# Residual and last tokens' phases of four batches turned on TensorE, with a new order of the whole program

## The chip, the cores and the metric

The kernel runs on one core of a Trainium2 chip. The metric is the device time of one execution in microseconds; lower is better. The engines are TensorE (PE in the profile), VectorE (DVE), ScalarE (ACT), GpSimd (POOL) and SyncE (SP), which here issues all transfers. Each works through its own queue in order.

## What is computed

An attention over 8 batches, 8 heads, 576 tokens and 64 channels a head, followed by a token-mixing block of width 512. Cut to what matters:

```python
q_d, k_d, v_d = means of q, k, v over groups of 4 tokens      # 144 tokens
out_d = softmax(q_d @ k_d.T / 8) @ v_d                        # repeated 4 times
out_local = softmax of q @ k.T / 8 where |i - j| < 4, @ v
x = out_up + out_local                                        # [8, 576, 512]

theta = x @ w_theta
zr, zi = x * cos(theta), x * sin(theta)
y = w_tok_r @ zr + w_tok_i @ zi                               # over tokens
u = x + y
out = u + maximum(u @ w_ch, 0)
```

## The kernel before

The program is written as small steps, each a function of a batch and a part, and the text `ORDER` names them one after the other: two letters for the step, then a place (a PSUM bank or a pair of banks, a staging buffer, or the engine: `v` VectorE, `a` ScalarE, `g` GpSimd). The loop at the end of the kernel walks over the words; each word takes the next instance of its step, so that the order within a step is fixed and the interleaving of steps is the text's. `pin` ties every instruction to the one before it on the same engine: the text is the order of every engine's queue. Eight batches go through it as a pipeline, with two buffers for most tiles. A word `wm` issues so many idle matmuls on a tile of zeros into a bank; they compute nothing.

The steps, in the order in which a batch meets them:

- `lk`, `lq`, `lv`/`lw` (L278, L330): loads of k, q and the two halves of v into one of 14 staging buffers. `ck`, `cq`, `cv` (L287, L341): their casts to bf16. `la`/`ca`, `lb`/`cb`, `lc`/`cc`, `wp`/`wc`: the weights.
- `tp` (L294): transposes of k and q on TensorE into a pair of banks; `ev` (L298): the copy out, into `kT`, `qT`.
- `kd`, `qd` (L304 to L318): the sums over 4 tokens. `sd`, `ed`, `nd`, `xn`, `xd`, `xc`: the coarse attention.
- `ps`, `ex`, `mk`, `po`, `nm` (L427 to L465): scores, exponential, mask, product with v and division of the local attention, in units of 116 tokens.
- `xt`, `xa` (L475, L481): x with channels on the partitions, `xT`.
- `th` (L492): theta of 128 tokens; `cs` (L497): cosine and sine. `tt`, `ct`: the same for the last 64 tokens, with channels on the partitions. `zt` (L513): their product with x, in `zT`.
- `dz` (L517): a transposing transfer turns `zT` into `z[:, 8, :]`, where tokens are on the partitions.
- `xm` (L523): x of 128 tokens turned on TensorE into a bank. For the batches in `XDMA`, here 6 and 7, `dx` (L526) does it by a transposing transfer into `xx`. `zz` (L530): x times cosine and sine, into `z`.
- `mx` (L546): the mixing over tokens, nine matmuls of 288 columns into a bank; `ua` (L551): plus x, into `uT`.
- `du` (L555): four transposing transfers a batch turn `uT` into `ur`, the residual with tokens on the partitions. `ut`, `dt`: the same for the last tokens of two batches.
- `ch` (L563): `u @ w_ch` of 128 tokens; `rl` (L568): the maximum with 0, plus `ur`, into one of five output buffers; `st` (L572): the store. `ht`, `rt`, `ss`, `sr`: the last tokens of two batches.
- `te`, `ts` (L643): a tiny activation that brings the table of exponential or sine onto ScalarE ahead of its use.

All matmul results lie in eight PSUM banks, which the words name.

Of the kernel before, what the change touches and what calls it, by code (L numbers as in the profile page):

```python
# [14 lines left out]
P = 128  # L15
B = 8
# [3 lines left out]
DM = 512  # L20
# [33 lines left out]
lb5 lb4 cba cbg cbg xn xt0 la6 lb7 cag nd67 la8 xt1 mk xn lb9 wm24 xd6 lba wp7 lbb lqc xca xt2 nm xt3 po45 cqg cbv caa  # L54
lkd xa lk0 caa wp6 ckg xa xa nm xm0 wca wp1 lq2 lk3 th7 ts cs cbg xa wcv xt2 lk5 th4 xa wp5 cbv tt3 xm2 cba ckg xm6 zz
wcv th7 cs wp4 xm0 zz ct wp1 lq4 tp23 wcv lq1 wp5 wcv lk7 cs cqv zt eva lq6 dz ckg th4 cs wp7 wcv wcv wp1 lq8 ckv zz
cqg lvc cqg wcv tp23 wcv tp45 tp67 eva kdg zz ckg mx1 lka eva mx0 cqv cqg ua eva ps23 lw kdv te ex ckg qdv ps45 ua lvb
ex mx1 mk tp67 tp23 lkd eva lk9 lw lv0 eva lw lv3 lv2 mx0 cvv po45 lw ua qdg ps67 mk lw mx1 nm cva ckg lq5 ckg tp23 ex
ua po45 kdv cvg nm sd67 eva ed lq4 mx0 sd23 qdg cva po45 ua cqg cqg ua nm mx6 cva lq1 lk6 ua lv7 mk pv01 kdg po45 wm71
po67 ed tp23 lk8 nm vda lva nm eva cka nd45 nd01 xt6 ps23 xn cqv qdg ckg lw cvg ps45 xn ex lqc mx7 lw lqd mk ua ps23  # L60
lk9 xd0 ex sd45 xt1 ex xcv xa ed cqg lvb tp23 xt0 xa xa ckg xt7 xt6 lk0 xa po45 cqg eva xa lw th1 ts cs xm0 tp23 tt7
th6 lq3 ct lv2 nm xm1 evv th4 xm5 lw th7 cs cs zt zz zz lv5 ckg xm6 dz tp23 cs eva cqv tp01 zz cvg po45 zz utg lk4 mk
mx7 mx6 qdg cvg po23 lw nm eva ua ps01 sd45 mx7 kdg lc6 ua te ed xt6 cvv ex mk nm cvg ua pv45 vda mk ps23 cka po01 lk1
lq8 nm mx7 kdg nd45 nd01 ua ex mx7 xn qdg lv7 lvc sd23 xn ps45 lw ua lc9 mk lw lvd lw lv0 du lva ed lw xt0 lw cvg xd1
xcv mx7 lq3 xa xt1 lcb ckg ex lk5 lc2 du xa xt4 cvg xa cca tp23 mx5 cva ua lv4 xa lq7 sd01 cqg ua eva cvg po67 nm po23
nm mx4 ed xt5 ua po01 th6 xa th7 nm ccv lk1 ts cs du po23 nm po45 du cqg cvg pv01 nm th6 xm2 tt3 ccg vda nd45 zz ckg
ct xn nd01 th2 xn cs tp45 ccv ckg xt3 xt7 zt xd0 lqc ch1 eva xcv cqg cs xa lw xa cqa xm0 xm4 lk8 kdg lk6 lvd lk0 lw
lk3 dz xt5 lka ch3 lvb tp67 cvg lw rl lq5 lq9 eva cs st ch1 xa rl zz ckv th5 ckg xt0 utv du du du du tp67 cs xm3 eva
cka zz th2 xa kdv mk ch0 cs zz th4 tp67 rl mx5 mx1 evv cs ps23 lq1 qdg ua po67 rl ua lv7 lv2 lq4 nm ps45 mx0 cqg xm1
cqv te ex xt6 xm7 mx2 lw mk ex ua ckg st cvg lw zz tp45 eva qdg tp01 xa tt3 mx6 mk zz th7 ua lk6 ts ct evv ua cvv lvc  # L70
lv8 xm2 cs lw lw zt ckg lv5 lw po45 sd01 cqa qdg lq0 ch3 ch6 nm st rl zz rl te ed xm7 mx3 du cvg zz cva ch2 dz ps45
# [21 lines left out]
def kernel(  # L93
# [11 lines left out]
    nc = tc.nc  # L105
# [40 lines left out]
    rl = tiles(2, [P, 2, 4], "rl", FP32)  # L146
# [23 lines left out]
    ident = one([P, P], "ident")  # L170
# [86 lines left out]
    at = {}  # L257
# [258 lines left out]
    def dz(b, w):  # L516
        nc.sync.dma_start_transpose(out=z[b % 2][:, 8, :].rearrange("p (e d) -> p e d", e=4),  # L517
                                    in_=zT.rearrange("p e r t -> p (e r t)"))

    def xm(b, c, w):  # L520
        ps = at["xm", b, c] = bank16(w)[:, 0:DM]
        for dc in range(4):
            nc.tensor.transpose(out=ps[:, P * dc:P * dc + P], in_=xT[b % 2][:, dc, P * c:P * c + P], identity=ident)  # L523
# [4 lines left out]
    def zz(b, c, w):  # L528
        x = xx[:, c, :] if b in XDMA else at.pop(("xm", b, c))
        nc.vector.tensor_tensor(out=z[b % 2][:, 2 * c:2 * c + 2, :],  # L530
# [22 lines left out]

    def du(b, dc, w):
        nc.sync.dma_start_transpose(out=ur[b % 2][:, :, P * dc:P * dc + P], in_=uT[b % 2][:, dc, 0:512])  # L555

    def ut(b, w):
        COPY[w](out=uts[b // 2 % 2][:, :, b % 2, :], in_=uT[b % 2][:, 0:4, 512:576])  # L558
# [35 lines left out]
    def span(*ns):  # L594
        out = [()]
        for n in ns:
            out = [x + (i,) for x in out for i in range(n)]
        return out

    STEPS = dict(  # L600
        k0=(lambda i, w: None, span(1)), kc=(kc, span(4)), la=(la, span(4)), ca=(ca, span(4)), lb=(lb, span(9)), cb=(cb, span(9)), lc=(lc, span(4)), cc=(cc, span(4)),
# [8 lines left out]
        zt=(zt, span(B)), dz=(dz, span(B)), xm=(xm, [(b, c) for b, c in span(B, 4) if b not in XDMA]), dx=(dx, [(b, c) for b, c in span(B, 4) if b in XDMA]), zz=(zz, span(B, 4)), mx=(mx, span(B, 8)),  # L610
        ua=(ua, span(B, 8)), du=(du, span(B, 4)), ut=(ut, span(B)), ch=(ch, span(B, 4)), rl=(rlf, span(B, 4)),
# [69 lines left out]
```

## Time and profile before

| | us |
|---|---|
| runs | 245.91, 248.43, 248.76 |
| median | 248.43 |
| the profiled execution | 247.32 |
| its span, first to last instruction | 245.6 |

| transfers, KB each | number | median us from issue to landing |
|---|---|---|
| halves of v, 128 | 80 | 5.6 |
| k, 288 | 32 | 5.4 |
| q, 288 | 32 | 4.8 |
| `du` | 32 | 3.8 |
| `dz` | 8 | 3.0 |
| `dx` | 8 | 2.5 |
| stores of output, 256 | 32 | 2.8 |

"Busy" sums the time in which an engine had an instruction; matmuls overlap in a pipeline, so that TensorE can be busy without being at its peak. A line names the line of the kernel, the engine, the tile written and the tiles read, with partitions and elements. In square brackets stands the idle time ahead of an instruction and what ended it. "issue" means that the profile shows nothing that the engine waited for. The chain of waits follows the work that ended last back to its releasers.

### The profile page before, as it was taken

To read this page: it belongs to the slowest core of one execution; us is meant where nothing else is said; L and a number is where in the kernel's file an instruction comes from. 1 tells how busy PE (TensorE), PEld (TensorE's weight loads), DVE (VectorE), ACT (ScalarE), POOL (GpSimd) and SP (SyncE) were. 2 spreads that over 40 slices of the span, in tenths; PEclk is the share of its full clock that TensorE was granted. 3 is DMA by queue.
4 is the path that set the end of the run, shared out by engine and by line. 5 is a ranking of instruction groups with operands and counts; after the bars stand their busy time and mean duration, and the time that the engine had idled before them with its cause. 6 is when DMAs were issued, how large, how long until landed. Compare 5 with 4: busy or idle time off the path is not lost.

```text
span 245.6 us, 8335 instructions
## 1 busy us (share of the span) xinstructions
PE 224.6 (91%) x3405; PEld 153.3 (62%) x3405; DVE 196.7 (80%) x410; ACT 155.7 (63%) x237; POOL 97.7 (40%) x143
## 2 busy tenths in 40 slices
PE   7998699797999789999988999999599999999992
PEld 2555467566777557686566687576367775677740
DVE  6479798797999879999878998888498888576472
ACT  3287598896997487988765579885756536800000
POOL 6361366569577353637078142119334000000000
PEclk9999999999999999999999999999999999999999
DMA  6999997899969999998999999899956395655577
GB/s 188 300 180 293 380 342 177 205 262 248 221 109 251 122 256 236 250 291 201 204 184 237 283 262 164 172 234 234 154 117 154 93 161 153 115 129 119 140 202 268
DMA packets 87494, 50.91 MB, mean 207 GB/s; under 512 B 72480, under 2 KB 72480, under 8 KB 87456
## 3 DMA queue, kind: packets, MB, share of 16 engines
q1 hardware_dynamic: 87456, 50.38, 92.9%
q8 instruction: 26, 0.43, 0.9%
q14 instruction: 12, 0.10, 0.1%
HBM read 34.11 MB, written 9.44 MB: 177 GB/s over the span
## 4 chain that ended last, share of the span: by engine, by line
PE 49%; DMA 21%; DVE 7%; ACT 7%; issue 5%; POOL 5%; SPq 4%; DVEq 0%; POOLq 0%; ACTq 0%
PE PS L546 17%; DMA st<-in_v_dram 13%; PE PS L563 8%; PE PS L492 7%; DMA st<-in_q_dram 4%; PE PS L294 3%; PE PS L638 3%; DMA st<-in_moe_w_tok_i_dram 3%; SPq L330 3%; POOL two L312 3%; PE PS L475 2%; PE PS L456 2%; DVE osb L568 1%; ACT cs L498 1%; ACT pm L435 1%
## 5 line engine op out<-in xcount | busy, mean ns | idle before, releaser
L546 PE MATMUL PS<-WT,z 128*128 128x288 bf16 x576 | 77.6, 286 | 1.7 <-DMA z<-zT 1.2
L546 PEld LDWEIGHTS <-z 128*128 128x128 bf16 x576 | 54.3, 98 | 17.0 <-DMA z<-zT 1.8
L551 DVE TENSOR_TENSOR uT<-PS,xT 128x288 bf16<-128x288 f32 x64 | 28.7, 452 | 13.7 <-PE PS L546 12.1
L492 PE MATMUL PS<-wth,xT 128*128 128x512 bf16 x128 | 32.1, 379 | 2.9 <-DVE osb L568 2.8
L563 PE MATMUL PS<-wch,uT 128*128 128x512 bf16 x128 | 31.1, 379 | 0.0
L465 DVE TENSOR_TENSOR tmp<-PS,rl 128x512 bf16<-128x512 f32 x40 | 27.7, 691 | 1.4
L568 DVE SCALAR_TENSOR_TENSOR osb<-PS,ur 128x512 f32<-128x512 f32 x32 | 21.8, 685 | 8.4 <-issue 3.6
L497 ACT ACTIVATE cs<-PS,pihc 128x512 bf16<-128x512 f32 x32 | 22.3, 697 | 9.0 <-PE PS L492 8.5
L341 POOL CAST v_w<-st 128x512 bf16<-128x512 f32 x22 | 14.2, 649 | 34.5 <-DMA st<-in_v_dram 34.3
L481 DVE TENSOR_TENSOR xT<-PS,xdT 128x464 bf16<-128x464 f32 (+1 forms) x40 | 23.8, 628 | 1.8 <-PE PS L475 1.7
L435 ACT ACTIVATE pm<-PS 128x1024 bf16<-128x1024 f32 (+1 forms) x24 | 20.5, 877 | 2.6 <-PE PS L427 2.5
L287 POOL CAST k_tm<-st 128x576 bf16<-128x576 f32 x19 | 13.2, 699 | 19.0 <-DMA st<-in_k_dram 18.9
L298 ACT COPY qT<-PS 128x1152 bf16<-128x1152 bf16 x14 | 15.8, 1131 | 7.5 <-PE PS L294 7.3
L558 POOL COPY ut<-uT 128x256 bf16<-128x256 bf16 x5 | 2.2, 437 | 45.4 <-DVE uT L551 45.4
L492 PEld LDWEIGHTS <-xT 128*128 128x128 bf16 x128 | 11.3, 98 | 13.5 <-issue 3.4
L312 POOL TENSOR_TENSOR two<-kT 128x580 f32<-128x580 bf16 x13 | 15.4, 1184 | 10.1 <-DVE kT L298 9.8
L643 ACT ACT_TABLE_LOAD x15 | 19.2, 1283 | 0.3
L498 ACT ACTIVATE cs<-PS 128x512 bf16<-128x512 f32 x32 | 19.4, 605 | 0.0
L563 PEld LDWEIGHTS <-uT 128*128 128x128 bf16 x128 | 11.8, 98 | 11.2
L382 ACT ACTIVATE pd<-PS 128x864 bf16<-128x864 f32 x16 | 14.0, 891 | 6.5 <-PE PS L371 6.4
L446 DVE TENSOR_TENSOR pm<-pm,band 128x1024 bf16<-128x1024 bf16 (+1 forms) x24 | 16.7, 696 | 1.3 <-ACT pm L435 1.3
L530 DVE TENSOR_TENSOR z<-PS,cs 128x1024 bf16<-128x1024 bf16 x24 | 16.2, 681 | 1.4 <-ACT cs L498 1.3
(95 smaller groups left out, 401.7 us busy)
## 6 DMA issues: line engine op xcount, KB each, us to landing
st<-in_v_dram SPq DMA_DIRECT2D x80, 128.0 KB, 5.6
st<-in_k_dram SPq DMA_DIRECT2D x32, 288.0 KB, 5.4
st<-in_q_dram SPq DMA_DIRECT2D x32, 288.0 KB, 4.8
out_dram<-osb SPq DMA_DIRECT2D x32, 256.0 KB, 2.8
st<-in_moe_w_tok_r_dram SPq DMA_DIRECT2D x4, 288.0 KB, 5.5
st<-in_moe_w_tok_i_dram SPq DMA_DIRECT2D x4, 288.0 KB, 6.6
st<-in_moe_w_theta_dram SPq DMA_DIRECT2D x4, 256.0 KB, 6.6
st<-in_moe_w_ch_dram SPq DMA_DIRECT2D x4, 256.0 KB, 4.5
```

The lines of the kernel that those rows point to most:

```text
L312: nc.gpsimd.tensor_tensor(out=t, in0=src[:, :, 0:2], in1=src[:, :, 2:4], op=ALU.add)
L435: nc.scalar.activation(out=pm[(3 * b + u) % NPM][:, :, 0:n].rearrange("p e c j w -> p e (c j w)"), in_=at.pop(("ps", b, u))[:, :, 0:4 * W ...
L465: nc.vector.tensor_tensor(out=tmp[(NCH * b + c) % NTMP].rearrange("p g (j d) -> p g j d", d=D), in0=ps[:, :, :, 0:D], in1=r.unsqueeze(3).t ...
L481: nc.vector.tensor_tensor(out=xT[b % 2][:, :, CH * c:CH * c + cnt].rearrange("p e (m j) -> p e m j", j=4), in0=at.pop(("xt", b, c))[:, :, ...
L492: nc.tensor.matmul(out=ps, lhsT=xT[b % 2][:, dc, P * c:P * c + P], rhs=wth[:, dc, :], start=(dc == 0), stop=(dc == 3))
L497: nc.scalar.activation(out=t[:, 0, :], in_=ps, func=AF.Sin, bias=pihc, scale=1.0)
L498: nc.scalar.activation(out=t[:, 1, :], in_=ps, func=AF.Sin, bias=0.0, scale=1.0)
L546: nc.tensor.matmul(out=ps, lhsT=z[b % 2][:, j, P * dc:P * dc + P], rhs=WT[:, j, cols], start=(j == 0), stop=(j == 8))
L551: nc.vector.tensor_tensor(out=uT[b % 2][:, dc, cols], in0=at.pop(("mx", b, i)), in1=xT[b % 2][:, dc, cols], op=ALU.add)
L563: nc.tensor.matmul(out=ps, lhsT=uT[b % 2][:, dc, P * c:P * c + P], rhs=wch[:, dc, :], start=(dc == 0), stop=(dc == 3))
L568: nc.vector.scalar_tensor_tensor(out=o, in0=at.pop(("ch", b, c)), scalar=0.0, in1=ur[b % 2][:, c, :], op0=ALU.max, op1=ALU.add)
L643: nc.scalar.activation(out=idle, in_=pihc, func=TABLE[kind])
```

## The change

There are four edits.

- `RPE = (0, 1, 2, 3)`: for these batches the residual `ur` is made by `up`, four TensorE transposes into a bank for each 128 tokens, and `uc`, the copy out of it, instead of the four `du` transfers of the batch.
- `ZPE = (0, 1, 2, 3)`: for these batches the last tokens' phases are turned by `zp`, four TensorE transposes, and `zc`, a copy, instead of `dz`.
- `XDMA = (7,)`: x of batch 6 is turned by `xm` on TensorE; only batch 7 still uses `dx`.
- `ORDER` is another text throughout: 1219 words for 1198. It holds 68 idle matmuls in 9 places for 53 in 10, 17 changes of ScalarE's table for 15, and other engines for some casts and copies (of 32 `ev` 10 on VectorE for 6; of 9 `wc` 4 on ScalarE for 1). It begins with four loads of q, where before two of k came first.

```diff
-XDMA = (6, 7)
+XDMA = (7,)
+
+RPE = (0, 1, 2, 3)
+ZPE = (0, 1, 2, 3)
...
-lk0 lk1 ckv cka lq2 wm0f tp01 evv lk3 cqa lk4 ckg lq5 lq6 cqv lq7 ckv wm2c tp23 lv8 k0 tp45 cqa cqa la9 wm62 tp67 eva
-kdg eva eva wm0a ps01 kcv caa lw lva lvb lvc ps23 kcv qdv cvg ex kcg lvd ex qdv kdg lw lw ps45 kcg lw wm62 sd67 mk
-wm03 po01 sd23 cvv lw lb0 cva nm po01 cvv cvv ex ed wm41 pv45 ed mk po67 la1 lb2 vda lb3 wm23 nd23 cbv po45 nm cbg nm
...
+lq0 lq1 cqg lq2 cqv lq3 cqv cqv lk4 lk5 cka ckv wm0z wm04 tp01 evv lk6 cka lk7 cka lv8 tp23 wm44 tp45 k0 tp67 lw lv9
+lw lva kcg kca evv evv eva wm06 ps01 ps23 lab kcv qdg lvc qdv kca lvd kdv kdg wm6a sd67 lb0 lw lw lw lb1 cva cvv ps45
+ex ex lb2 mk ed cva sd01 ex cvg wm21 po23 mk po67 caa cvg lb3 ed la4 po45 pv01 la5 cba vda lb6 nm nm caa xt6 xt7 la7
...
+    def zp(b, w):
+        ps = at["zp", b] = bank16(w)[:, 0:DM]
+        for ec in range(4):
+            nc.tensor.transpose(out=ps[:, P * ec:P * ec + P], in_=zT[:, ec, :, :], identity=ident)
+
+    def zc(b, w):
+        COPY[w](out=z[b % 2][:, 8, :], in_=at.pop(("zp", b)))
...
+    def up(b, c, w):
+        ps = at["up", b, c] = bank16(w)[:, 0:DM]
+        for dc in range(4):
+            nc.tensor.transpose(out=ps[:, P * dc:P * dc + P], in_=uT[b % 2][:, dc, P * c:P * c + P], identity=ident)
+
+    def uc(b, c, w):
+        COPY[w](out=ur[b % 2][:, c, :], in_=at.pop(("up", b, c)))
...
-        zt=(zt, span(B)), dz=(dz, span(B)),
...
+        zt=(zt, span(B)), dz=(dz, [(b,) for b in range(B) if b not in ZPE]),
+        zp=(zp, [(b,) for b in ZPE]), zc=(zc, [(b,) for b in ZPE]),
+        up=(up, [(b, c) for b in RPE for c in range(4)]), uc=(uc, [(b, c) for b in RPE for c in range(4)]),
...
```

More of the change, by code (lines that the diff above doesn't have):

```diff
@@ L55 @@
[L55 to L59, printed above, removed]
@@ new lines @@
+zz evv zca tp45 mx0 lv6 lw lv8 lv9 cqv lw lvb tp23 eva wm11 tp67 evv eva lw lw lka kdg lkc mx1 ps45 qdg ps23 lqd qdg
+mx6 cvv lq0 ua te ex kdv ua mx7 ua lk4 cvg ex ps01 mk po45 cvg ua sd23 lk5 lq1 sd67 ex ed po01 ckg nm cva up4 mk mx5
+ed po23 nm cvv pv01 vda lq2 lc7 ua nm ckg lv3 po67 lw uca cqa mx5 lc6 lv8 nd23 nd01 lw nm cqg up4 lv9 uca lw lvb lw
+tp67 ua xt5 xn xt2 xn eva xt3 xd4 tp01 eva mx6 cka mk xcv xa xt7 cqg po45 xa xa th2 th3 nm lva kdg lqc xt4 ckg ts cs
+xa th5 lw xm2 cqv xa cs xm4 cvg tt7 qdg zz cs ua ct zz th0 zt lkd xm1 tp23 cs ccg tp45 eva xm6 mx7 zz zp0 zz evv zca
@@ new lines @@
+mx6 ps23 qdv te ex ua ps01 ua mx4 ex cva mx5 mk cvv po23 ua kdg cvg cqg sd67 ed sd01 mk lk0 mx4 ed nm cvg pv67 vda cka
+lq1 lc4 ua lc2 lq5 ua po23 nm po01 lk3 mx5 nd23 nm cca lq7 xn lqb lkc ckg nd67 tp01 mx4 ccg xn xd6 ccg lva lw lv9 ua
+eva cqa ps23 ex cqa xcv po01 lk8 nm ch5 tp67 mk eva lv0 xt0 rl xt1 lq4 xa xa ch2 kdg xt3 cka lkd lv2 po67 lv6 xt5 th0
+ts cs cqg xa nm lw lk1 cqg th3 ckv xa rl xt1 qdg tp67 xa xm5 th0 ua th1 cs up4 cs evv tp23 lw tt0 ckg xm6 zz evv mx5
+lw up7 lw utg cs ct lk5 lq7 lqb kdg ps01 ps23 ucv cqv ua cvg zz te ex ucv ex ch4 up5 ckg up6 qdg tp01 xm7 xm2 cvg ckg
@@ new lines @@
+lv3 zt eva rl uca lw lqc lv8 zp3 mk ch4 lva tp01 zca zz ucv rl zz eva mx5 cvv sd67 cvg po23 ed ua nm ps01 ch4 sd67 st
+cvg lk4 po23 ex lkd mk ed pv01 mx5 vda nm mk up2 ckg tp67 utv uca rl nd01 ua cqg nd45 cqv eva tp23 xn lw eva xn mx6
+up7 ua kdg lw kdg po01 ps45 nm ex po23 lq9 mx6 ps01 nm po45 xd2 xca lk1 mx3 xt2 ucv ckg nm ua cqv xt7 xt6 xa mk cqg xa
+ch4 xa mx2 xt5 cvv ex xa qdg lk2 cka lv6 xt7 qdg rl th6 th5 cvv tp01 xa th4 lw ua ts cs cs tt3 evv tp67 cvg cvg cs ua
+lv5 st ckv eva ct th5 xm4 cs st po01 ckg lw mk zz kdg cvg nm mx2 ua ch3 lk0 sd67 lq7 cqg lqb cqg lq4 po01 nm te ed
@@ new lines @@
+ct lvb po01 mx6 du xd7 up2 lw xt3 qdg ua xcv th4 ua mk th5 xm7 dt uca zt cs xm2 xa cs dz nm zz ch3 cvv lv4 st zz xt4
+po01 ps67 te ex mx5 nm xa mx2 kdg mk xt4 ua mx6 cvg xa du th7 lvc st xt5 ts cs rl xt3 mk lw mx4 lw ua ua ua th2 cs xa
+mx4 xa du ht5 po01 ua nm ps67 sd23 rt mx4 te ex cva ed ua mk cvv mx0 po67 po45 nm nm pv23 ch1 st mx6 vda st xm7 sd45
+ua rl po23 po01 ua zz ed th6 tt7 nm nd45 nd23 nm th0 ch1 xn xn xd2 xt3 ss xm4 utg zz du xt5 ts ct ch7 xca utv rl cs du
+xa rl xt4 ht2 ch1 xt3 xt6 sr st zt du cs ch0 xa xa th7 xa th3 xm5 xa du xm4 ch6 st rl st st cs dz dx zz dx zz mx1 mx7
@@ L609 @@
         xa=(xa, span(B, NCH)), th=(th, span(B, 4)), cs=(csf, span(B, 4)), tt=(tt, span(B)), ct=(ct, span(B)),
[L610 to L611 removed]
+        zt=(zt, span(B)), dz=(dz, [(b,) for b in range(B) if b not in ZPE]),
+        zp=(zp, [(b,) for b in ZPE]), zc=(zc, [(b,) for b in ZPE]),
+        up=(up, [(b, c) for b in RPE for c in range(4)]), uc=(uc, [(b, c) for b in RPE for c in range(4)]),
+        xm=(xm, [(b, c) for b, c in span(B, 4) if b not in XDMA]), dx=(dx, [(b, c) for b, c in span(B, 4) if b in XDMA]), zz=(zz, span(B, 4)), mx=(mx, span(B, 8)),
+        ua=(ua, span(B, 8)), du=(du, [(b, c) for b, c in span(B, 4) if b not in RPE]), ut=(ut, span(B)), ch=(ch, span(B, 4)), rl=(rlf, span(B, 4)),
         st=(st, span(B, 4)), dt=(dt, span(4)), ht=(ht, span(4)), rt=(rt, span(4)), ss=(tail_store(0), span(4)), sr=(tail_store(1), span(4)),
```

46 lines of the change are left out of this document (16 added, 30 removed).

## The prediction

> **What bounds the kernel now.** I read the page first, then the busy times by stage, the chain of waits through the middle, the waits of TensorE, and last the groups and single lines that price the edits.
>
> ```profile
> span 245.6 us, 8335 instructions
> ...
> PE 224.6 (91%) x3405; PEld 153.3 (62%) x3405; DVE 196.7 (80%) x410; ACT 155.7 (63%) x237; POOL 97.7 (40%) x143
> ```
>
> ```profile
> core 0: us, PE busy (x) PEld busy (x) DVE busy (x) ACT busy (x) POOL busy (x), PEclk, DMA share, GB/s
> 0.00:40.00 40.00, 35.53 (x469) 21.08 (x469) 30.45 (x80) 25.27 (x38) 19.90 (x44) 1.00 0.98 270
> 40.00:180.00 140.00, 128.37 (x2280) 92.08 (x2278) 119.91 (x243) 108.73 (x164) 72.38 (x92) 1.00 1.08 216
> 180.00:220.00 40.00, 40.00 (x529) 27.04 (x527) 31.97 (x64) 21.68 (x37) 5.04 (x7) 1.00 0.60 130
> ```
>
> The 91% of TensorE is an average over unlike stages. From 180 us on it is never idle (40.00 of 40). From 40 to 180 it is idle for 140.00 - 128.37 = 11.6 us, and there the DMA share is 1.08, over 1 because packets overlap. The same transfers per us later on (130 against 216 GB/s) come with 0.60. What fills the queues in the middle is therefore the suspect for the 11.6 us. The chain of waits over 40 to 137 us agrees, its first two entries being loads:
>
> ```profile
> by line: DMA st<-in_v_dram 32.3%; DMA st<-in_q_dram 10.8%; PE PS L492 6.4%; SPq L330 6.4%; POOL two L312 6.4%; issue 5.6%; PE PS L546 3.6%; PE PS L563 3.6%; SPq L278 2.8%; POOL kd L315 2.4%; PE PS L294 2.1%; POOL v_w L341 2.1%; PE PS L456 1
> ```
>
> What reaches TensorE of this is in its own waits (engine and line, who was waited for, total, times, longest):
>
> ```profile
> PE PS L492 <- DVE osb L568: 2.8, 1, 2.8
> PE PS L294 <- POOL k_tm L287: 2.6, 2, 1.8
> PE PS L456 <- ACT kT L298: 1.3, 1, 1.3
> PE PS L217 <- DVE warm L188: 1.3, 1, 1.3
> PE PS L427 <- ACT pm L435: 1.2, 1, 1.2
> PE PS L546 <- DMA z<-zT: 1.2, 1, 1.2
> ```
>
> Two of them are transposing transfers: the last by name (dz, late behind other words of the SP queue), and the first at one remove. There VectorE stood 3.19 us with no releaser named, at an rl, and TensorE waited for that rl:
>
> ```profile
> 169.85 1.30 SPq L555 DMA_TRANSPOSE ur<-uT  x1
> ...
> 175.29 0.69 DVE L568 SCALAR_TENSOR_TENSOR osb<-PS,ur 128x512 f32<-128x512 f32 x1 [3.19 <-issue]
> ...
> 176.04 1.02 PE L492 MATMUL PS<-wth,xT 128*128 128x512 bf16 x4 [2.80 <-DVE osb L568]
> ```
>
> The rl reads ur, which du fills; the du issued at 169.85 us is the sixteenth, the last of batch 3. In the stage from 130 to 180 us a du took this long to land:
>
> ```profile
> ur<-uT SPq DMA_TRANSPOSE x9, 4.8
> ```
>
> So I read that 2.80 as a wait for a du; the row alone does not prove it. The transfers thus hold 2.8 + 1.2 = 4.0 us of the 11.6. The waits for k_tm, kT and pm (2.6 + 1.3 + 1.2 = 5.1 us) come after casts and copies that share an in-order engine with casts of loads, and I count them to the loads. About 2.5 us are small waits.
>
> **What TensorE gains in work.** Added are 16 up (residual of batches 0 to 3), 4 zp and 4 more xm (batch 6), each of four 128x128 transposes: 24 x 4 = 96.
>
> ```profile
> 14.11 2.16 PE PS L638 x10
> ...
> 96.97 0.45 PE PS L523 x8
> ```
>
> Eight transposes advance the chain by 0.45 us, so one takes 0.056, and 96 x 0.056 = **+5.4 us**. A group's mean of 219 ns for L523 is latency, of which the next one hides most. Where TensorE is full there is no cover, and I charge all of it. A rule speaks against this price, and stands by itself: the Trainium skill, TensorE: Matmul & The Clock Gate, Part 4 (PE-mode transpose), gives about 275 ns for one in a kernel and says that such work does not count as busy for the clock gate. The row above disagrees on the price, and the granted clock of 1.00 in the stages above, which hold transposes of k, q and x, shows no loss of clock.
>
> **What the DMA queue loses.** 16 du, 4 dz and 4 dx go.
>
> ```profile
> L555 SPq DMA_TRANSPOSE ur<-uT x32: 1192/1262/2855, 80.8 to 234.2; - x32
> ```
>
> At the median of 1.262 us each, 24 x 1.262 = 30 us of SP's queue are free, and no load waits there behind a du that waits for uT. SP itself is not the end of the chain; its worth is in the waits. Gone with du and dz of batches 0 to 3 are the 4.0 us (the du is batch 3's, and so is the dz, the fourth): **-4.0**. Bounds: 0, if the copy that takes the transfer's place is as late, and -4.0. I take the whole, because a copy takes 0.45 to 0.63 us (below) where the du took 4.8 to land. The dx of batch 6 fell into the stage where TensorE is never idle; without them nothing is gained there, and the four xm are in the 5.4.
>
> **The copies.** The turned tiles come out of PSUM by 16 uc (8 VectorE, 8 ScalarE) and 4 zc (1 and 3). The nearest rows are the copies of 128x576:
>
> ```profile
> L269 DVE COPY WT<-PS x8: 441/448/459, 31.1 to 38.7; 128x576 bf16<-128x576 bf16 x8
> L269 ACT COPY WT<-PS x1: 632/632/632, 28.9 to 28.9; 128x576 bf16<-128x576 bf16 x1
> ```
>
> That is at most 9 x 0.448 = 4.0 us of VectorE and 11 x 0.632 = 7.0 of ScalarE. The new list also moves casts and copies: four ev go from ScalarE to VectorE.
>
> ```profile
> L298 ACT COPY kT<-PS x12: 1111/1118/1194, 13.3 to 160.6; 128x1152 bf16<-128x1152 bf16 x12
> L298 DVE COPY kT<-PS x4: 1342/1352/1358, 9.2 to 180.3; 128x1152 bf16<-128x1152 bf16 x4
> ```
>
> That adds 4 x 1.352 = 5.4 to VectorE and takes 4 x 1.118 = 4.5 from ScalarE. VectorE loses three wc (1.3), a kd (1.35, taken as an ev) and two cc (0.9, taken as wc) and gains a vd (about 1.0, two or three such copies); its casts of k and q nearly cancel. That is +6.9 in all. ScalarE has two more table changes:
>
> ```profile
> L643 ACT ACT_TABLE_LOAD x15: 1283/1283/1283, 29.6 to 195.6; - x15
> ```
>
> With 7.0 - 4.5 + 2 x 1.28 it stands at +5. Between 40 and 180 us VectorE has 20.1 us idle and ScalarE 31.3, and that is the cover: I take **0**. Bounds: 0, and +6.9 if VectorE's queue paces that stage. A gain below 0 I exclude, since nothing here shortens a queue. Each up and zp holds one of the eight PSUM banks until its copy, and TensorE's next user of that bank waits; behind a waiting transpose everything on TensorE is queued. In the list a uc follows its up by 2 to 25 words; at 245.6 us for 1198 words (0.205 us a word) that is 0.4 to 5 us, so most have time.
>
> **The new order in the middle.** A load gives TensorE no wait when it stands far enough ahead of its cast. I counted words between lk and ck, lq and cq, and lw and cv, for batches 1 to 7 (91 pairs). Under 25 words (25 x 0.205 = 5.1 us, about the landing of a load) there were 27 before and there are 12 after; the median goes from 36 to 44. Waits of loads: at least 5.1 x 15/27 = 2.8 us go, at most all 5.1. I take **-5.1**, the end to which the longer median leads point, as the 24 transposing transfers also leave the same queues.
>
> **The head.** Ahead of the first transposes stand 39 idle matmuls where there were 15, and 67 where there were 52 ahead of the first th.
>
> ```profile
> 8.52 0.67 PE L294 MATMUL PS<-ident,k_tm 128*128 128x128 bf16 x9
> ...
> 30.02 1.04 PE L492 MATMUL PS<-wth,xT 128*128 128x512 bf16 x4
> ```
>
> With 2.16 us for ten, the first transposes move from 8.52 by 24 x 0.216 = 5.2 to 13.7 us. The first th need not move so far, since k was only one of its causes. From 13.7 VectorE's queue in the new list has, up to the second xa: three ev and two means (5 x 1.35), one cvv, 2.5 mk, five nm, two xn, a copy and two xa.
>
> ```profile
> L465 DVE TENSOR_TENSOR tmp<-PS,rl 128x512 bf16<-128x512 f32 x40 | 27.7, 691 | 1.4
> L481 DVE TENSOR_TENSOR xT<-PS,xdT 128x464 bf16<-128x464 f32 (+1 forms) x40 | 23.8, 628 | 1.8 <-PE PS L475 1.7
> L568 DVE SCALAR_TENSOR_TENSOR osb<-PS,ur 128x512 f32<-128x512 f32 x32 | 21.8, 685 | 8.4 <-issue 3.6 <-DMA out_dram<-osb 3.3 <-PE PS L563 1.5
> L446 DVE TENSOR_TENSOR pm<-pm,band 128x1024 bf16<-128x1024 bf16 (+1 forms) x24 | 16.7, 696 | 1.3 <-ACT pm L435 1.3
> L530 DVE TENSOR_TENSOR z<-PS,cs 128x1024 bf16<-128x1024 bf16 x24 | 16.2, 681 | 1.4 <-ACT cs L498 1.3
> L403 DVE TENSOR_TENSOR xdn<-PS,rd 72x512 bf16<-72x512 f32 x16 | 11.0, 687 | 0.5
> L464 DVE RECIPROCAL rl<-PS 128x8 f32<-128x8 f32 x40 | 8.0, 199 | 2.9 <-PE PS L456 2.6
> ```
>
> With 0.89 for nm and xn (0.691 + 0.199; 0.687 for the xn's product) that is 6.8 + 0.4 + 1.7 + 4.5 + 1.8 + 0.4 + 1.3 = 16.9 us; from the end of the first transposes at 14.3, 31.2 us, against 30.02 now. Overlap of neighbours would shorten it. Bounds: 0 and 15 x 0.216 = 3.2; I take **+1.0**.
>
> **The sum** goes against the profiled execution: 247.32 us, 1.72 more than its span of 245.6. It lies between the runs shown (245.91 to 248.76, median 248.43), 1.1 under the median. 245.6 + 5.4 - 4.0 - 5.1 + 0 + 1.0 = 242.9 us of span, and with the 1.72, **244.6 us**: 1.5% under the median. With each term at its worse bound but the copies' (5.4, 0, -2.8, 3.2) it is 253.1; with the better ones (5.4, -4.0, -5.1, 0) it is 243.6.
>
> **The rivals.** *All idle time of the middle goes* (0.30). Its small waits have the same source and go too, and the head loses nothing: 245.6 + 5.4 - 11.6 = 239.4, with the rest 241.1 us. For it speak the DMA share of 1.08 and the leads; against it that most of the small waits of TensorE name VectorE and no transfer.
>
> *The waits only change their name* (0.11). TensorE waits 4.0 us for copies in place of transfers, and of the loads' waits only 2.8 go: 245.6 + 5.4 + 1.0 - 2.8 + 1.72 = 250.9 us. The change then would do what it says and leave the time where it was.
>
> *VectorE becomes the pacer* (0.20), the slower one. Between 40 and 180 us it is 119.91 of 140 us busy, 86%, and its idle time is where it waits for TensorE. With its 6.9 us more in order ahead of the operations for which TensorE waits, both pay: 245.6 + 5.4 + 6.9 + 1.0 - 4.0 + 1.72 = 256.6 us. It decides from the point at which VectorE's share there passes some 92%; for it speaks that the groups shown above, L568 apart, have under 3 us of idle time before them, so that VectorE is mostly held by its own queue; against it, that 20.1 us of idle time are there to take 6.9.
>
> *The transposes cost TensorE what a lone one takes* (0.01). With L523's 0.219 us each in place of 0.056, 96 x 0.163 = 15.6 more: 260.2 us. The row of eight in 0.45 us is against it. By the Trainium skill's 275 ns, as cited above, it would be some 21 us more, an estimate.
>
> **How the numbers follow.** The forecast has 0.38; its own range is 242 to 249, from the better bounds with half of the small waits gone besides to a loss of some 4 us on the terms that were taken at their better ends, and a third of its weight lies under 243.5. A difference of 2%, 5.0 us, is about what a measurement of this kernel can tell from no change, so faster means under 243.5 us and slower over 253.4. Faster: 0.30 + 0.12 = 0.42. Slower: 0.20 + 0.01 and 0.01 of the renamed waits at their upper end, 0.22. Within: 0.36. The range goes from 239.5, under the first rival, to 254; left out are most of VectorE's case (0.14) and 0.04 below. Faster and slower together hold most of the chance; the likeliest case's own range is the 242 to 249 above.
>
> **What would show it.** In the new profile L555 has 16 transfers and none before batch 4; no osb waits 3 us on "issue" while batches 0 to 3 last. TensorE's idle time between 40 and 180 us falls from 11.6 us to some 2 to 5. The first th stands near 31 us; past 33 the head is mis-sized. The new transposes advance the chain by 0.22 us for four. If the copies' cover fails, TensorE's waits list uc, zc or xT by VectorE with several us, and VectorE's share in the middle is over 92%. The forecast is wrong at its base if loads still head the chain of the middle with their 43%, or if TensorE's idle time there is as long as before with other names on it.

## The result, and the profile after

| | before | after |
|---|---|---|
| median of 20 runs each, us | 249.46 | 248.28 |
| lowest and highest | 244.63 to 255.24 | 247.75 to 250.03 |
| profiled execution | 247.32 | 248.22 |
| its span | 245.6 | 246.5 |

The ratio of after to before is 1.007, with a 95% interval from 1.0041 to 1.0098: within 2%, and if anything slightly slower, where the forecast was 244.6 us and faster. The ratio leaves out disturbed runs, of which the kernel before had more, and so it lies above 1 although the median of all runs is lower. The changed kernel scatters far less than the one before. The versions below were run in groups, each beside the kernel before, whose median there lay between 247.35 and 248.04 us where it is 249.46 here; the changed kernel itself was not run again. Versions are compared with its 248.28 us by their own medians, and across groups a difference of one or two microseconds is not told from none. The ratio to the kernel before is given as well.

The page of the changed kernel, busy times of the engines:

```profile
span 246.5 us, 8526 instructions
...
PE 229.9 (93%) x3487; PEld 160.6 (65%) x3516; DVE 206.1 (84%) x416; ACT 160.8 (65%) x252; POOL 101.1 (41%) x146
```

TensorE is busy for 5.3 us more. That this is near the 5.4 foreseen is luck: it holds 15 more idle matmuls, and 29 matmul records are missing from this profile (3487 for 3516 weight loads). VectorE has 9.4 more, and it was to have 6.9. The busy times by stage (columns as in the prediction) say where:

```profile
0.00:40.00 40.00, 35.09 (x434) 20.50 (x438) 29.71 (x71) 23.09 (x40) 17.93 (x40) 0.96 1.02 268
40.00:180.00 140.00, 133.49 (x2415) 99.14 (x2428) 130.01 (x251) 113.05 (x170) 81.21 (x103) 1.00 0.82 194
180.00:220.00 40.00, 39.53 (x501) 26.69 (x506) 31.78 (x66) 24.68 (x43) 1.52 (x3) 1.00 0.53 136
```

Between 40 and 180 us the DMA share fell from 1.08 to 0.82, and TensorE's idle time from 11.6 to 6.5 us (140.00 - 133.49). The missing records make that somewhat too much: `head15` below, the same program in this stage and with all its records, shows 5.3. Had the 9.1 us of the terms "-4.0" and "-5.1" simply gone, 2.5 would be left. VectorE went from 119.9 to 130.0 us, 93% of the stage. TensorE's waits of the changed kernel, here over the whole execution, name it almost throughout (engine and line, who was waited for, total, times, longest):

```profile
PE PS L460 <- DVE pm L450: 1.3, 2, 0.7
PE PS L221 <- DVE warm L192: 1.3, 1, 1.3
PE PS L460 <- DVE tmp L469: 1.1, 2, 0.7
PE PS L415 <- DVE xdn L407: 1.0, 1, 1.0
PE PS L353 <- ACT pd L386: 1.0, 1, 1.0
PE PS L558 <- DVE xT L485: 0.7, 1, 0.7
PE PS L535 <- DVE xT L485: 0.6, 1, 0.6
```

The 2.8 us behind an `rl` and the 1.2 for `z` are gone, casts of k, q and v hold it for 0.2 us each, and no transfer stands in the list. What replaced them are short waits for the mask (`pm`), the division (`tmp`) and `xT`: operations that the change did not touch. They stand in a queue that is longer. Between 40 and 180 us TensorE's waits name VectorE for 5.2 us, in 14 waits of which none is over 0.7; before, it was 4.5 us in 7, of which 2.8 were the one `rl`. The chain of waits from 40 to 180 us has the same in it; loads of v and q, which led it before, are not among its first entries:

```profile
by line: PE PS L558 18.6%; issue 7.2%; PE PS L298 5.4%; PE PS L583 5.4%; DVE xT L485 4.5%; PE PS L496 4.2%; DVE pm L450 3.8%; DVE kT L302 3.8%; PE PS L460 3.3%; DMA st<-in_k_dram 3.1%; DVE q_tm L291 2.8%; DVE uT L563 2.3%; PE PS L535 2.1%; 
```

The first thetas, in the timeline of TensorE, start at 31.73 us for 30.02:

```profile
31.73 3.63 PE L496 MATMUL PS<-wth,xT 128*128 128x512 bf16 x16
```

### The profile page after: what moved, and what is told of

Same layout as the page of the kernel before. It is cut to its first block, busy times and chain, and to the rows that moved or that the text cites. A ratio compares the mean times of both kernels' runs of the same rounds, so it can differ in the third digit from the quotient of the medians.

```text
span 246.5 us, 8526 instructions
## 1 busy us (share of the span) xinstructions
PE 229.9 (93%) x3487; PEld 160.6 (65%) x3516; DVE 206.1 (84%) x416; ACT 160.8 (65%) x252; POOL 101.1 (41%) x146
## 4 chain that ended last, share of the span: by engine, by line
PE 59%; DVE 18%; DMA 9%; issue 5%; SPq 4%; ACT 2%; POOL 1%; DVEq 0%; ACTq 0%
PE PS L558 22%; PE PS L583 9%; PE PS L496 7%; DMA st<-in_moe_w_tok_i_dram 3%; PE PS L298 3%; DVE xT L485 3%; DMA st<-in_v_dram 3%; SPq L334 3%; PE PS L460 2%; DVE pm L450 2%; DVE kT L302 2%; PE PS L535 2%; PE PS L479 2%; PE PS L269 2%; DMA st<-in_k_dram 2%
## 5 line engine op out<-in xcount | busy, mean ns | idle before, releaser
L558 PE MATMUL PS<-WT,z 128*128 128x288 bf16 x576 | 78.6, 286 | 1.0 <-DVE xT L485 0.7
L558 PEld LDWEIGHTS <-z 128*128 128x128 bf16 x576 | 54.1, 98 | 16.9 <-issue 1.9
L563 DVE TENSOR_TENSOR uT<-PS,xT 128x288 bf16<-128x288 f32 x64 | 27.9, 449 | 7.2 <-PE PS L558 6.8
L583 PE MATMUL PS<-wch,uT 128*128 128x512 bf16 x115 | 30.2, 379 | 1.0 <-issue 0.3
L496 PE MATMUL PS<-wth,xT 128*128 128x512 bf16 x117 | 29.9, 379 | 1.1 <-issue 0.3
L316 POOL TENSOR_TENSOR two<-kT 128x580 f32<-128x580 bf16 x14 | 16.3, 1166 | 32.4 <-ACT kT L302 17.3
L485 DVE TENSOR_TENSOR xT<-PS,xdT 128x464 bf16<-128x464 f32 (+1 forms) x40 | 23.9, 628 | 1.9 <-ACT xdT L419 0.9
L542 DVE TENSOR_TENSOR z<-PS,cs 128x1024 bf16<-128x1024 bf16 x28 | 18.9, 682 | 3.6 <-PE PS L535 2.8
L316 POOL TENSOR_TENSOR two<-qT 128x576 f32<-128x576 bf16 x13 | 14.9, 1144 | 14.4 <-DVE qT L302 9.0
L345 POOL CAST v_w<-st 128x512 bf16<-128x512 f32 x24 | 15.7, 665 | 9.6 <-issue 5.5
L496 PEld LDWEIGHTS <-xT 128*128 128x128 bf16 x128 | 11.5, 98 | 11.9 <-DVE xT L485 1.2
L302 ACT COPY qT<-PS 128x1152 bf16<-128x1152 bf16 x12 | 13.4, 1119 | 8.4 <-PE PS L298 7.4
L583 PEld LDWEIGHTS <-uT 128*128 128x128 bf16 x128 | 11.6, 98 | 10.8 <-issue 0.6
L450 DVE TENSOR_TENSOR pm<-pm,band 128x1024 bf16<-128x1024 bf16 (+1 forms) x24 | 18.0, 755 | 0.2 <-ACT pm L439 0.2
```

Source lines behind the costliest of these rows:

```text
L316: nc.gpsimd.tensor_tensor(out=t, in0=src[:, :, 0:2], in1=src[:, :, 2:4], op=ALU.add)
L450: nc.vector.tensor_tensor(out=t, in0=t, in1=m, op=ALU.mult)
L485: nc.vector.tensor_tensor(out=xT[b % 2][:, :, CH * c:CH * c + cnt].rearrange("p e (m j) -> p e m j", j=4), in0=at.pop(("xt", b, c))[:, :, ...
L496: nc.tensor.matmul(out=ps, lhsT=xT[b % 2][:, dc, P * c:P * c + P], rhs=wth[:, dc, :], start=(dc == 0), stop=(dc == 3))
L558: nc.tensor.matmul(out=ps, lhsT=z[b % 2][:, j, P * dc:P * dc + P], rhs=WT[:, j, cols], start=(j == 0), stop=(j == 8))
L563: nc.vector.tensor_tensor(out=uT[b % 2][:, dc, cols], in0=at.pop(("mx", b, i)), in1=xT[b % 2][:, dc, cols], op=ALU.add)
```

## The experiments

Two suspects stood at the outset: the head (the later first theta), and VectorE, with ScalarE as the rival for the copies. Further runs asked what the turning and the order are worth alone.

### The head: `head15`

```diff
-wm0z
+wm0b
```

The block of 35 idle matmuls ahead of the first transposes becomes one of 11, so that 15 stand there as before.

> The changed kernel with 15 idle matmuls ahead of the first transposes in place of 39 (the word wm0z becomes wm0b); all else as it was. Theory H (the idle matmuls hold the head: the casts of the first k ended at 8.40 us, the first transposes began at 12.42, and VectorE stood 4.72 us): the first transposes at 8.5 to 8.9, the first theta product at 28 to 29 in place of 31.7, and 245 to 246 us in place of 248.3. Rival (the weights' casts, which end at 28.0, and the loads hold the head anyway): first theta product not before 31, 247.8 to 248.5 us.

Measured: 246.93 us (10 runs, 246.11 to 250.13), ratio 1.0087 (1.0055 to 1.0119). TensorE's timeline of the changed kernel,

```profile
12.42 0.67 PE L298 MATMUL PS<-ident,k_tm 128*128 128x128 bf16 x9
```

and of `head15`:

```profile
9.43 0.66 PE L298 MATMUL PS<-ident,k_tm 128*128 128x128 bf16 x9 [2.03 <-DVE k_tm L291]
...
31.72 1.47 PE L496 MATMUL PS<-wth,xT 128*128 128x512 bf16 x6
```

The first transposes come 3.0 us earlier (9.43 for 12.42), the first theta not at all (31.72 for 31.73). Two rows of `head15`, of ScalarE and of TensorE, show where two thirds of the lead go:

```profile
20.02 0.62 ACT L345 CAST v_w<-st 128x512 bf16<-128x512 f32 x1 [1.16 <-DMA st<-in_v_dram]
```

```profile
21.18 0.31 PE L460 MATMUL PS<-v_w,pm 64*64 64x65 bf16 x9 [1.95 <-ACT pm L439]
```

ScalarE waits for a load of v, the exponential stands behind that cast in its queue, and TensorE waits for the exponential. This is the rival of the expectation (no theta before 31 us), though the time lies between the two ranges. The median is 1.3 us better than the changed kernel's (and 1.7 better than that of `uc_act`, run beside it), but its ratio to the kernel before is no better. The idle matmuls ahead of the first transposes hold at most some 1.3 of the 3.7 us by which the forecast missed.

### Which engine carries the copies: `uc_act` and `uc_vec`

```diff
 uc_act: the eight ucv and the zcv of the list
-ucv
+uca
-zcv
+zca
 uc_vec: the eight uca and three zca
-uca
+ucv
-zca
+zcv
```

> The changed kernel with the 8 uc and the one zc of VectorE moved to ScalarE. Theory V (VectorE's queue paces the stage from 40 to 180 us, where it is 93% busy): its 4 us less there show almost whole, 245 to 246.5 us, and VectorE's share there falls. Rival E (that stage is held by TensorE's own work and by short chains between engines, whoever copies): within 1 us of 248.3; or slower by 1 to 3 us because ScalarE, 113 of 140 us busy, takes 5 us more.

> The changed kernel with the 8 uc and 3 zc of ScalarE moved to VectorE, which makes its queue longer by some 5 us. Theory V: 3 to 5 us longer, 251 to 253.5 us. Rival E: within 1 us of 248.3.

With all copies on ScalarE: 248.6 us (10 runs), ratio 1.0102 (1.0059 to 1.0146). With all on VectorE: 250.51 us (4 runs), ratio 1.0174 (1.0082 to 1.0266). Eleven more copies at 0.414 us are 4.6 us of VectorE, and half of that came out in the time (250.51 for 248.28). The other direction gains nothing: VectorE's time in the middle fell only from 130.0 to 127.7 us, while each copy moved from 0.414 us to 0.594 on ScalarE (their median in `uc_act`), and the bank is held as much longer. By the expectations `uc_act` falls to the rival and `uc_vec` lies between the two, so this pair does not settle it.

### Relief of VectorE by GpSimd: `casts_pool`, and the same in the kernel before: `before_pool`

```diff
 casts_pool: in the middle of the list, 6, 3 and 6 words
-cqv
+cqg
-ckv
+ckg
-cvv
+cvg
```

`before_pool` does the same with 17 such casts of the old list.

> The changed kernel with 15 casts of q, k and v in the middle (6 cq, 3 ck, 6 cv) moved from VectorE to GpSimd, which takes some 9 to 10 us from VectorE's queue and gives as much to GpSimd (81 of 140 us busy there). Theory V: 3 to 6 us shorter, 242 to 245.5 us, limited by the 11 us that TensorE's work leaves open in that stage. Rival E: within 1 us of 248.3, or longer, where the casts on GpSimd come later than they did on VectorE.

> The kernel before with 17 casts of q, k and v (from batch 1 on) moved from VectorE to GpSimd, as in casts_pool. If the relief of VectorE is worth the same there, 3 to 4 us under the kernel before; theory V says that it is worth less there, 0 to 2 us, since VectorE was 86% busy in the middle and the waits were those of loads and transfers; or it is a loss, where GpSimd's casts hold up what it does for the loads.

`casts_pool`: **244.2 us** (10 runs, 243.61 to 246.16; its slowest run is under the changed kernel's fastest), ratio 0.9999 (0.995 to 1.0048). Its stage from 40 to 180 us:

```profile
40.00:180.00 140.00, 137.29 (x2499) 102.00 (x2501) 123.78 (x236) 116.38 (x176) 89.83 (x119) 1.00 0.82 195
```

6.2 us less on VectorE (123.78 for 130.01) brought TensorE's idle time from 6.5 to 2.7 and the time down by 4.1 (4.4 under `uc_act`, run beside it; by the ratios, which carry the scatter of the kernel before, only 0.7%, some 1.8 us). TensorE's waits of this stage:

```profile
PE PS L460 <- POOL v_w L345: 1.2, 1, 1.2
PE PS L572 <- DVE tmp L469: 0.5, 1, 0.5
PE PS L460 <- DVE tmp L469: 0.4, 1, 0.4
PE PS L396 <- DVE osb L588: 0.2, 1, 0.2
PE PS L460 <- DVE z L542: 0.2, 1, 0.2
```

VectorE is named for 1.3 us where it was 5.2, and that difference is about the gain. The span is 242.7; the prediction's sum, which charges the copies at nothing, is 242.9. In the chain of the same stage TensorE's own lines now lead:

```profile
by line: PE PS L558 26.1%; PE PS L496 12.5%; PE PS L298 7.5%; PE PS L583 6.9%; DMA st<-in_k_dram 4.3%; PE PS L460 3.7%; PE PS L479 3.3%; DMA z<-zT 2.9%; DVE pm L450 2.9%; PE PS L535 2.7%; PE PS L431 2.3%; PE PS L396 2.2%; issue 2.2%; PE PS 
```

`before_pool`: 246.91 us (10 runs) beside 247.42 for the kernel before, ratio 0.9987 (0.994 to 1.0034): nothing that can be told, though up to 1.5 us would fit. Its row for that stage shows VectorE relieved as much. The execution profiled took 250.97 us, 4 over the median, so TensorE's idle time in it (11.9 us) is not that of a typical run:

```profile
40.00:180.00 140.00, 128.14 (x2252) 92.29 (x2266) 113.98 (x218) 108.50 (x163) 83.36 (x109) 0.98 1.03 215
```

So VectorE's load cost the changed kernel some 4 us and the kernel before little or nothing. The move also frees the casts' place in VectorE's queue, where a late load would hold what is behind it; the next pair takes work away that needs no load.

### Relief without a load: `mask_off` and `before_mask_off`

```diff
     def mk(b, u, w):
+        if 1 <= b <= 5:
+            return
```

> The changed kernel without the mask's multiplication in batches 1 to 5 (it leaves that part of the local attention out): 15 instructions of VectorE, some 10 us, are gone, and nothing is added on another engine. Theory V: 242 to 245 us, and TensorE's idle time between 40 and 180 us falls from 6.5 to under 4 us, as it did in casts_pool. Rival C (casts_pool gained by the place of its casts, not by a shorter queue of VectorE): 247 to 248.5 us.

> The same left out of the kernel before. Theory V says that its middle was held by waits for loads and transfers and not by VectorE: 0 to 2.5 us under the kernel before, less than mask_off gains. If VectorE's length counts as much there: 3 us or more.

`mask_off`: 244.43 us (9 runs, 244.0 to 246.08), ratio 0.991 (0.9872 to 0.9948), by either count some 4 us under the changed kernel. VectorE has 7.0 us less in the middle; TensorE is idle for 4.8 us, not under 4 as expected, in an execution that was the longest of the nine (246.08):

```profile
40.00:180.00 140.00, 135.22 (x2453) 100.08 (x2451) 123.03 (x240) 114.02 (x172) 78.92 (x105) 1.00 0.80 196
```

`before_mask_off`: 247.64 us (10 runs) beside 247.5 for the kernel before, ratio 0.9966 (0.9913 to 1.002). Again the same relief is worth 3.9 us in the changed kernel and nothing that can be told in the old one, where the interval leaves room for some 2 us. So the gain needs no cast and no load.

### Both reliefs together: `pool_mask_off`

> The changed kernel with its 15 casts of the middle on GpSimd and, besides, without the mask of batches 1 to 5, so that those batches' local attention is left without its band. Each alone gave about 4 us (244.2 and 244.4 for 248.3). If both gave it by one thing, VectorE's queue, which then is no longer what TensorE waits for, the two together give little more than one: TensorE was idle for 2.7 us of the middle with the casts away, so 242 to 244. If they are two separate costs (the casts' own loads and buffers, and the mask's place between exponential and product with v), they add: 240.3, with TensorE's idle time in the middle gone altogether and some gained outside it.

242.66 us (4 runs), ratio 0.9846 (0.9766 to 0.9927): 1.5 us under `casts_pool`, where two separate costs would have given 3.9. The two act on the same thing, and once VectorE's share in the middle is down to 88% (123.78 of 140) most of its price is gone. The profiled execution was the longest of the four (245.52 us), so its rows are not used.

### The rival engine: `act_pool`

```diff
 18 casts of the middle
-cqa
+cqg
-cka
+ckg
-cva
+cvg
```

> The changed kernel with 18 casts of q, k and v in the middle moved from ScalarE (not VectorE) to GpSimd: 12 us off ScalarE's queue, VectorE's as it was. Theory V (VectorE alone paces the middle): 247.5 to 249 us, no gain. Theory VA (both queues pace it, which is why moving the copies from one to the other gave nothing): 245 to 246.5 us.

249.98 us (7 runs), ratio 1.0072 (1.0037 to 1.0106): 1.7 over the changed kernel by the median, the same by the ratio, though ScalarE lost 10.5 us of the stage:

```profile
40.00:180.00 140.00, 132.51 (x2387) 98.13 (x2403) 129.97 (x249) 102.56 (x149) 90.97 (x120) 1.00 0.85 195
```

Relief of ScalarE gains nothing, so its queue is not what paces TensorE here. Nor is it merely that casts on GpSimd are good: moved from ScalarE they bring nothing. (Less than 2 us could hide behind VectorE's casts, which that move slows; last section.)

### The price of a transpose: `up_twice`

```diff
-            nc.tensor.transpose(out=ps[:, P * ec:P * ec + P], in_=zT[:, ec, :, :], identity=ident)
+            for _ in range(2):
+                nc.tensor.transpose(out=ps[:, P * ec:P * ec + P], in_=zT[:, ec, :, :], identity=ident)
```

The same is done in `up`; each of the 80 new transposes is issued twice.

> The changed kernel with every transpose of up and zp issued twice into the same place, 80 more transposes, 80 x 0.056 = 4.5 us of TensorE. Theory P (TensorE is full, so its added work is paid whole): 252 to 253 us. Theory V (in the stage from 40 to 180 us VectorE paces and TensorE has 6.5 us of idle time): 248.3 to 250 us.

251.31 us (4 runs), ratio 1.0182 (1.0113 to 1.0252), between the two expectations: +3.0 us for 80, or 0.038 each where 0.056 was charged. At lone prices (0.219) it would have been 17.5. In the chain of this run eight still take 0.45 us, and TensorE's idle time from 40 to 180 us is 5.2 us where it was 6.5, so part of them was covered. TensorE's busy time gives a like price: `uc_act`, with the work of the changed kernel and all its records, has 231.8 us, 7.2 over the kernel before; less 15 idle matmuls at 0.216, some 4 us are left for 96 transposes (an estimate).

### Turning and order apart: `du_back`, `before_turned`, `before_turned_late`

`du_back` is the new list with the 16 transfers in place of `up` and `uc`, each some ten words behind its sums:

```diff
-RPE = (0, 1, 2, 3)
+RPE = ()
```

> The changed kernel and its order with the residual of batches 0 to 3 turned by du transfers again, each placed some ten words after the sums that it reads; the 16 up and 16 uc are left away, which takes 64 transposes (3.6 us) from TensorE, 3.6 us of copies from VectorE and 5 us from ScalarE. Theory V: VectorE's stage gets 3.6 us back and the time falls by 2 to 4 us, to 244 to 246.5, although the transfers are back. Theory D (the turned residual earned what the prediction gave it, waits of 2.8 us and lighter queues, and was eaten by other parts of the change): 250 us or more.

257.51 us (4 runs), ratio 1.0444 (1.0357 to 1.0531), 9.2 over the changed kernel and within theory D (250 us or more): what VectorE saves by eight copies fewer does not pay for the transfers. Its waits (all engines; lines stand one lower) hold what the prediction had read in the old profile, larger:

```profile
POOL v_w L344 <- DMA st<-in_v_dram: 29.2, 9, 7.4
...
DVE osb L587 <- DMA ur<-uT: 7.5, 3, 5.4
```

and among those of TensorE:

```profile
PE PS L395 <- DVE osb L587: 6.0, 2, 5.5
```

TensorE waits 5.5 us for an `rl` that waits 5.4 for a `du`: the same two-step wait, this time with the transfer named. Part of it belongs to this kernel alone, since the new list puts the `rl` of batch 1 11 words behind its last `du`.

`before_turned` and `before_turned_late` are the old list with the residual and phases of batches 0 to 3 turned on TensorE (`XDMA` stays (6, 7)); in the first an `up` stands 6 to 12 words behind its sums, in the second at least 16. In the second an idle matmul of the list overwrites the bank of the first `up`, so the residual of 128 tokens of batch 0 is not the real one.

> The kernel before, its order, its idle matmuls and its x of batches 6 and 7 by transfers, with only the residual and the last tokens' phases of batches 0 to 3 turned on TensorE (each up set where its sums are ready and a bank is free, its uc 7 to 12 words later, the copies shared 8 and 8 by VectorE and ScalarE, zc on ScalarE). Theory D (the turned tiles earn the 4.0 us of transfer waits and free SP's queue, against 80 x 0.056 = 4.5 us of TensorE and VectorE has room in this order): 245 to 247.5 us, at most 1 us from the kernel before. Rival (the old order is held by its loads, so that TensorE's 4.5 us lie partly in their waits and lighter queues speed the loads): 242 to 245 us. Rival (the copies hold VectorE up here too): 249 us or more.

> The old order with the residual and the last tokens' phases of batches 0 to 3 turned on TensorE, as in the run before it with the early places, but each up now stands 18 words or more after the sums that fill its uT, and each zp 7 or more after its phases. If the cost of that run (some 6 us over the kernel before) came from TensorE waiting at up and zp for operands that were not ready (PE L572 on DVE tmp 3.3 us, PE L527 on DVE zT 1.2), turning alone costs its 80 transposes at 0.056, 4.5 us, less the 4.0 of the transfers' waits: the kernel before + 0 to 2 us, 247.5 to 250, with no wait of TensorE at L572 over 0.7 us. If the copies themselves hold VectorE and ScalarE, which in the old order is no pacer (86% of the middle), the time stays where it was, 252 to 254, with TensorE's waits naming uc, zc or the operations behind them.

They took 253.87 us (4 runs; ratio 1.022, 1.0155 to 1.0285) and 260.49 us (4 runs; ratio 1.0514, 1.0393 to 1.0635). The first falls by its number to the rival of 249 us or more, but VectorE, with 119.7 us from 40 to 180 us, is no busier there than before (119.9). The second was expected at 247.5 to 250 or at 252 to 254, so both theories miss. TensorE's waits, first in the early one, then in the late one:

```profile
PE PS L572 <- DVE tmp L469: 3.3, 4, 1.5
PE PS L661 <- ACT pm L439: 1.5, 1, 1.5
PE PS L353 <- DVE ur L575: 1.3, 1, 1.3
...
PE PS L527 <- DVE zT L517: 1.2, 1, 1.2
```

```profile
PE PS L572 <- DVE tmp L469: 2.6, 4, 1.4
PE PS L572 <- DVE xT L485: 2.3, 3, 1.0
PE PS L535 <- DVE xT L485: 1.7, 1, 1.7
PE PS L535 <- ACT z L530: 1.6, 1, 1.6
PE PS L460 <- ACT ur L575: 1.3, 1, 1.3
```

The waits for transfers are down to 0.4 us in both (for a `z`), and what came are waits at the new steps themselves. At L572 TensorE waits less for `uT` (0.9 us in the late one) than for `tmp` and `xT`, so for the earlier reader of the bank into which it turns; at L460 and L353 the next user of a bank waits for the copy out of it. The later place put the steps among other users of the banks. What turning alone is worth is therefore not settled by these two: each list prices its own places. They do show that the transposes and copies can cost far more than their own time, and that the new list has room for them where these two have not.

### The version that beats both: `pool_head15`

`casts_pool` and `head15` together.

> casts_pool and head15 together. head15 began its transposes 3 us earlier and had lost all of it by the first theta product (31.72 us in both), so it should add nothing to casts_pool: 243.5 to 244.5 us. If the head counts after all, 242 to 243 us.

**243.12 us** (4 runs, 242.79 to 244.85), ratio 0.9868 (0.9792 to 0.9944): 1.1 under `casts_pool`, 5.2 under the changed kernel. The shorter head counts for about as much as it did alone, which across groups is little more than can be told; the ratios (0.9868 against 0.9999) point the same way.

## Why the prediction was wrong

**What bounds the kernel: right.** The waits for loads and transfers held TensorE in the old middle, and after the change no transfer is in its list. `du_back` shows the wait at one remove that the prediction had only read from "issue". That loads held the rest is read from the rows; no run tests it alone.

**The transposes, +5.4: a little too high.** The 80 extra of `up_twice` cost 3.0; at that price 96 cost 3.6 us. They were charged without cover, and some of them found it in TensorE's idle time (6.5 to 5.2 us in that run).

**The transfers, -4.0, and the loads, -5.1: gone by name.** Their sizes were not measured apart. That the sum holds once VectorE is relieved (span 242.7 for 242.9) supports the four terms +5.4, -4.0, -5.1 and +1.0 together, not each; that it holds to 0.2 us is partly luck, since the first was some 1.8 too high and the last 0.7 too low.

**The copies, +0: here the prediction failed.** "Between 40 and 180 us VectorE has 20.1 us idle and ScalarE 31.3, and that is the cover: I take 0": for ScalarE that held (`act_pool`), for VectorE's 6.9 us of new work it did not. Two things were off. The new work was 10.1 us in that stage, since casts and masks became slower as well (last section). And the idle time was not all cover: VectorE works in the order of the list, 9.2 of the 20.1 us ended with something from TensorE, and the operations for which TensorE waits next stand in the same queue. The step was some +4 and not 0. With VectorE filled from 86% to 93%, about 4 us came back as TensorE's waits of a few tenths each: `casts_pool` takes back 4.1, `mask_off` 3.9, and TensorE's waits for VectorE fall from 5.2 to 1.3 us in the former. That is inside the step's bounds, 0 to +6.9; the lower end was taken as the value.

**The rival that came true in kind** is "VectorE becomes the pacer", by its own point (92% in the middle) and its own sign in the profile (waits for `xT`). Its price was too high: 256.6 us charges all of the 6.9 and brings back the loads' waits besides, where 4 were paid and the loads stayed away. A share just over the point buys only part of the price. "The waits only change their name" came nearer to the time (250.9 for 248.28) than the forecast, but by the wrong names: neither `uc` nor `zc` is in TensorE's list. It is what stands behind them.

**The head, +1.0:** the first theta came 1.7 us later, so the size was a little off, but that it was near is luck. The reason given, 16.9 us of VectorE's queue from the end of the first transposes, fails in `head15`: transposes 3.0 us earlier should have brought the theta 3.0 earlier, and moved it by 0.01. In its place a load of v and the exponential behind it took most of the lead; what holds the rest of the head stays open.

In sum: 245.6 + 5.4 - 4.0 - 5.1 + 1.0 is the 242.9 of the prediction; with 4 for VectorE it is 246.9, and with the head's 0.7 more 247.6, against 246.5 measured. The 1.1 over is no more than the transposes' cover (5.4 - 3.6 = 1.8). The sum starts from one execution of a kernel whose runs lie between 244.63 and 255.24 us, so closer agreement would prove nothing.

## What to carry to other kernels

Do not count an engine's idle time as cover for new work where it waits for the very engine that will wait for it in turn. Here VectorE, at 86%, took 10.1 us more, and some 4 of them were paid; ask which operations stand behind the new work. When a change removes a wait and the time stays, see whose name TensorE's short waits bear now, relieve that engine by work that has nothing to do with the change, and do the same in the old kernel: a gain in the one and none in the other names the new bound. A change that moves work between engines is finished only when the casts that any engine can do have been shared out anew.

## What of the hardware was not expected

VectorE's instructions took longer without having changed. Its groups between 40 and 180 us, those with operands in SBUF alone, before and after:

```profile
L446 DVE TENSOR_TENSOR pm<-pm,band 128x1024 bf16<-128x1024 bf16 (+1 forms) x18 | 13.1, 729 | 0.4 <-ACT pm L435 0.3
L287 DVE CAST q_tm<-st 128x512 bf16<-128x512 f32 (+1 forms) x10 | 5.6, 597 | 0.3 <-DMA st<-in_q_dram 0.3
L341 DVE CAST v_w<-st 128x512 bf16<-128x512 f32 x6 | 2.5, 418 | 1.5 <-DMA st<-in_v_dram 1.5
L287 DVE CAST k_tm<-st 128x512 bf16<-128x512 f32 (+1 forms) x8 | 2.1, 303 | 0.3 <-DMA st<-in_k_dram 0.3
```

```profile
L450 DVE TENSOR_TENSOR pm<-pm,band 128x1024 bf16<-128x1024 bf16 (+1 forms) x17 | 13.7, 808 | 0.2 <-ACT pm L439 0.2
L291 DVE CAST q_tm<-st 128x512 bf16<-128x512 f32 (+1 forms) x12 | 7.2, 643 | 0.0
L345 DVE CAST v_w<-st 128x512 bf16<-128x512 f32 x6 | 3.9, 644 | 0.0
L291 DVE CAST k_tm<-st 128x512 bf16<-128x512 f32 (+1 forms) x6 | 3.6, 633 | 0.0
```

42 instructions for 23.3 us became 41 for 28.4. At the old means the 41 would last 23.9, so some 4.5 of the 10.1 us are slower instructions and not more of them (the shapes in each group are mixed as before). Groups that read PSUM kept theirs: `tmp` 691 and 692 ns, `xT` 628 and 628. The timelines of VectorE and of GpSimd of the changed kernel show one such case:

```profile
112.28 1.13 DVE L450 TENSOR_TENSOR pm<-pm,band 128x1024 bf16<-128x1024 bf16 x1
```

and on GpSimd beside it:

```profile
111.71 1.16 POOL L345 CAST v_w<-st 128x512 bf16<-128x512 f32 x2
112.82 1.12 POOL L291 CAST k_tm<-st 128x576 bf16<-128x576 f32 x1
```

A mask that takes 0.69 us at 71.90 took 1.13 beside two casts of GpSimd, and the second of these 1.12, where others of its kind take 0.66. The mask at 71.90 began 0.07 us ahead of a GpSimd cast of k and kept its time; there it was the cast that took 1.15. The Trainium skill, SBUF — State Buffer, section "Who interferes with whom", states that a VectorE instruction with two inputs in SBUF and a GpSimd instruction that reads SBUF contend, that one in a 2-port mode, which a cast can enter, and one of GpSimd shut each other out, and that a VectorE instruction with at most one SBUF input outside these modes does not contend. The rows above agree: masks and casts slowed, `tmp` and `xT` did not. GpSimd was busy for 81.2 us of the stage where it had been for 72.4. `act_pool` leaves VectorE's list as it was and brings GpSimd to 91.0: the same 41 instructions then take 29.8 us for 28.4, though the masks among them are a little faster (788 ns), so GpSimd's busy time alone does not set it. Which instructions met was followed only in the cases above. In `casts_pool`, with 89.8, the masks slowed further, to 868 ns in the mean, and the kernel still gained: the casts that left VectorE weigh more than what the others lost. The GpSimd share of the new work on VectorE was in no term of the sum.
